# A new written order of steps and output products in a convolution and SwiGLU kernel

## The chip, the cores and the metric

The kernel runs on one core of a Trainium2 chip. A core has TensorE (matrix products, PE in the profile, with its weight loads as PEld), VectorE (DVE), ScalarE (ACT), GpSimd (POOL) and SyncE (SP), which here only issues transfers; each works through its own queue in order, and semaphores make one wait for another. The metric is the time of one execution on the device, in microseconds (us); lower is better.

## What is computed

The input x has 8 sequences of 4096 tokens with 192 channels. A causal convolution of 7 taps runs over each of 8 heads of 24 channels, its weights a softmax over the taps. Each token is then scaled by its root mean square and goes through a gated feed-forward layer with 1536 hidden channels, all in float32:

```python
w = np.exp(weight - np.max(weight, axis=-1, keepdims=True))
w = w / (np.sum(w, axis=-1, keepdims=True) + 1e-09)
out = np.einsum('hk,bskhg->bshg', w, x_unf)       # x_unf: the 7 last tokens of each token
rms = np.sqrt(np.mean(x * x, axis=-1, keepdims=True) + 1e-06)
xn = x / rms * rms_g
g = xn @ w_gate
val = xn @ w_val
return (silu(g) * val @ w_out).astype(np.float32)
```

## The kernel before

**Tiling.** The 32768 tokens are cut into 32 pairs of two tiles of 512 tokens. Pair 0 is computed plainly, with preparation of the weights in between; pairs 1 to 31 run through the loop at line 1437. What follows is about these 31.

**Fewer products by sums.** A 3 by 3 block product takes 15 products of sums of blocks where 27 would be plain, once for the two input projections and once for the output projection.
- *Chain* (`CHAINS`, line 801): 4 units of three hidden blocks, together 60 entries (unit, result v, product i), each for two halves h: h = 0 is the gate on partitions 0 to 63, h = 1 the value on partitions 64 to 127. One entry and half is one step, two matmul instructions of 64x512 (line 839). A pair has 120 such steps, 240 instructions. Their right-hand sides are the slots 0 to 15 of the tile `xa`: six fetched blocks and sums of them. Slots 12 and 13, and 10 and 14, hold sums for the other half of the partitions; `swap` (line 707) copies them there with two transfers each: `swA` from slots 6 and 11, `swB` from slots 8 and 9. In unit 0 the second entry reads slot 14, the fifth slot 12, the sixth slot 13.
- *Output products* (`OUTS`, line 93): 60 products named form.unit, for instance 13.3; 15 forms, 4 units. Each is 8 matmul instructions of 128x256 (line 1024). `LEFT` (line 934) says what each form reads: hidden blocks a to f, or the sums AB, CB, X and S, which are built up in place as the products go by (`SUMS`: abe adds e to AB between forms 8 and 13, abd adds d between forms 13 and 2).

**PSUM.** Eight banks, four per half. A chain result takes a bank when it starts, and gives it back when it has been read; the output accumulators N, R, K, C01 and C34 take banks in the same way. `F` steps fork a result: they copy one bank into another, from which a second sum goes on (`FORK`, line 808: F0 starts result 0 from result 1, F3 starts result 3 from result 5).

**The order.** `ORDER` (line 98) is a list written out by hand, one for all pairs. Its first letter is the engine: V and W VectorE, A ScalarE, G GpSimd, P VectorE with an operand staged in PSUM by the Ak step of the same name, Q a GpSimd transfer that adds as it lands, D a transfer. `p3` lets TensorE go on by three: chain steps first, then output products. A trailing `-` means that the step belongs to the pair before. Kinds of chain steps: S save, F fork, C, D, R, N sums, G Silu, M product of gate and value, with v, half and unit behind. `AF3.1.3` is so the fork of result 3, half 1, unit 3, on ScalarE. Of the output part: S8, S2 and others save a bank, D0 to D13 add saved banks, T0 to T5 transpose a finished accumulator into the output tile, `st0` and `st1` store it. The convolution of the pair after next runs along: `cv3_1` is tap 3 of third 1 (`part_tap`, line 462; the accumulator lies in the half that `SIDE` names), then sq, red, pre, pow, dup, bc, mul, place. X0 to X6 (line 714) build the sums of `xa` for the next pair: X2 makes slot 6, X3 slot 11, X5 slot 8, X6 slot 9, and `fetA`, `fetB` fetch its blocks.

**The last pair** has no successor, so `last` (line 1383) rewrites the order for it: the steps in `NEEDS` come as soon as what they need is there.

The order says in which sequence each engine meets its instructions. When one of them starts is settled by its engine's queue and by what it waits for.

Of the kernel before, what the change touches and what calls it, by code (L numbers as in the profile page):

```python
# [19 lines left out]
def kernel(  # L20
# [36 lines left out]
    PAIRS = B * NB  # L57
# [33 lines left out]
    PLACE = {'a': 3, 'b': 4, 'c': 5, 'd': 0, 'e': 1, 'f': 2}  # L91
    BANKS = {'K': 1, 'R': 0, 'N': 0, 'C01': 0, 'C34': 1}
    OUTS = (
        "6.2 11.2 6.0 6.1 11.0 11.1 6.3 4.0 11.3 4.1 4.2 9.1 14.0 14.3 14.1 4.3 9.2 9.0 9.3 8.1",
        "8.3 5.0 5.2 5.1 5.3 8.0 3.1 7.0 8.2 10.2 7.1 10.0 3.3 3.2 10.3 7.3 7.2 14.2 10.1 13.0",
        "1.1 13.2 1.2 12.0 12.3 12.2 12.1 13.3 13.1 3.0 1.3 1.0 0.3 0.0 0.1 2.0 0.2 2.1 2.3 2.2",
    )
    ORDER = (
        "Vcv4_1- p2 VT2- DswA- VD1- Vcv5_1- VT4- Vcv6_1- p1 AS2- VT1- AS40.0.0 p1 VD2- VT0- VT5-",
        "VD3- AS40.1.0 p1 AF0.0.0 Asq- p2 VT3- p1 VC.0.0 VF0.1.0 AS41.0.0 AS41.1.0 p1 VC.1.0 p2",  # L100
        "Vred- AS00.1.0 AS00.0.0 p2 VD5.0.0 AS42.0.0 p1 VD5.1.0 p4 VR0.0.0 Apre- p1 AS42.1.0 p1",
        "AS51.0.0 p1 AS51.1.0 p1 AF2.0.0 VR1.0.0 VR0.1.0 AG0.0.0 AG1.0.0 p2 VN.1.0 p2 VR1.1.0",
        "VR2.0.0 VR2.1.0 AF3.0.0 AF3.1.0 p3 AS44.0.0 p2 Gpow- AG2.0.0 VR3.0.0 AS44.1.0 p1 VR3.1.0",
        "p1 AS40.0.1 GM0.1.0 p1 GM2.1.0 AS40.1.1 VR5.1.0 AG4.0.0 Gdf.0 Adup- AF0.0.1 p1 AS41.0.1",
        "VR5.0.0 p2 AG3.0.0 VM4.1.0 VF0.1.1 p2 VC.0.1 AS41.1.1 p1 VC.1.1 AS00.0.1 p3 AG5.0.0",
        "GM1.1.0 GM3.1.0 VS00.1.1 AS42.0.1 AS42.1.1 p1 Vbc- VD5.0.1 p1 Qde.0 p1 VD5.1.1 AS51.0.1",
        "VR1.0.1 VR1.1.1 AS51.1.1 p2 Gmul- AF2.0.1 p1 Dload- p2 VR0.0.1 p2 AF2.1.1 p1 Gab.0 p2",
        "AG0.0.1 VR0.1.1 VR2.0.1 GM0.1.1 AF3.0.1 VR2.1.1 AF3.1.1 p3 AG2.0.1 p1 GM2.1.1 VS44.0.1",
        "p1 VR3.0.1 VR3.1.1 AS44.1.1 GM5.1.0 AS40.0.2 AS40.1.2 p1 AG4.0.1 VR5.0.1 p3 Gcb.0",
        "AF0.0.2 AG1.0.1 p1 VR5.1.1 VM4.1.1 VS41.0.2 VS41.1.2 p2 AF0.1.2 AG5.0.1 VC.0.2 Dplace-",  # L110
        "p1 VC.1.2 AS00.0.2 p1 GM1.1.1 p1 GM5.1.1 VS42.0.2 p1 Gdf.1 p1 AS00.1.2 p2 AG3.0.1 p1",
        "VD5.0.2 p1 AS42.1.2 VR1.0.2 VD5.1.2 AS51.0.2 p1 AF2.0.2 p1 AS51.1.2 VR1.1.2 VR0.0.2",
        "Gp4.0 Dst0- AF2.1.2 p2 AG1.0.2 GM3.1.1 p2 AG0.0.2 VR0.1.2 VF3.0.2 VR2.0.2 AF3.1.2 p1",
        "VR2.1.2 p1 AS44.0.2 p1 AG2.0.2 Qde.1 GM1.1.2 AS44.1.2 p3 AS40.0.3 VR5.0.2 GM0.1.2",
        "VR5.1.2 p1 GM2.1.2 p1 VR3.0.2 AS40.1.3 VR3.1.2 AG4.0.2 p2 AF0.0.3 Gdf.2 p1 VM4.1.2",
        "AF0.1.3 p1 VS41.0.3 p3 Gab.1 p1 AG3.0.2 p1 AS41.1.3 p1 VC.0.3 p1 AG5.0.2 AS00.0.3 p1",
        "VC.1.3 AS00.1.3 AS42.1.3 p1 GM3.1.2 p2 VS42.0.3 VD5.0.3 VD5.1.3 AS51.0.3 p1 VR1.0.3 p1",
        "AS51.1.3 p2 AF2.0.3 p1 GM5.1.2 Gde.2 VR1.1.3 p1 Gac.2 AG1.0.3 Dst1- VR0.0.3 VR0.1.3 p1",
        "AF2.1.3 p1 AS44.0.3 p1 AG0.0.3 GM1.1.3 VF3.0.3 p1 VR5.0.3 AF3.1.3 p1 AS44.1.3 VR2.0.3",
        "GM0.1.3 p1 DfetA VR2.1.3 VR3.0.3 AG2.0.3 GM2.1.3 WR3.1.3 Akp4.1 Pp4.1 p2 Gdf.3 AG5.0.3",  # L120
        "Gde.3 WR5.1.3 Akp4.2 AG4.0.3 p3 Akcb.1 VM4.1.3 AG3.0.3 Akab.3 p1 Pcb.1 p2 Pp4.2 VM3.1.3",
        "VM5.1.3 p1 Pab.3 p2 Akp9.2 p1 AF3 p1 Pp9.2 Gp9.1 p1 Akp4.3 p2 Acv0_0 Gcb.3 Gp9.0 Pp4.3",
        "Akp9.3 p1 Vcv1_0 p2 Qbe.0123 Pp9.3 Acv0_2 Vcv2_0 Vcv1_2 p1 Akbce.0 AF1 p2 AF0 Vcv3_0 p1",
        "Vcv2_2 p2 Vcv4_0 AS6 Pbce.0 p2 Qabe.13 Vcv5_0 p2 AS5 p1 Vcv3_2 Gbce.1 p2 AkX0 PX0 p2",
        "Akabe.0 p1 Gbce.23 Vcv6_0 p1 Vcv4_2 p1 Akabe.2 AS8 Pabe.0 Vcv5_2 Gbcf.01 Pabe.2 p1 AkX3",
        "p2 PX3 DfetB Vcv6_2 p3 AkX1 Gbcf.3 p1 Akbcf.2 AS7 p1 AkX4 PX1 Acv0_1 p2 Pbcf.2 p3 Qabd.0",
        "GX5 PX4 p1 VD7 p1 AkX6 AF4 p1 Vcv1_1 GX2 PX6 p2 Vcv2_1 p1 Gabd.13 AS13 p2 DswB p2 Gabd.2",
        "p2 VD6 Vcv3_1 VD0 VD13",
    )

    cst = ctx.enter_context(tc.tile_pool(name="cst", bufs=1))
# [4 lines left out]
    outs = ctx.enter_context(tc.tile_pool(name="outs", bufs=2))  # L136
# [785 lines left out]
    def out_sums():  # L922
# [4 lines left out]
            )  # L927
            yield

    SIDE = (1, 1, 1)  # L930
    regs = held[0 : 2 * NU] + [more[:, i] for i in range(2)]
    REG = {"AB": 0, "CB": 1, "X": 2, "S": 3}

# [22 lines left out]
        "T0": ("C0", 0, 0), "T1": ("C1", 0, 1), "T2": ("N", 0, 2),  # L956
        "T3": ("C3", 1, 0), "T4": ("C4", 1, 1), "T5": ("K", 1, 2),
    }

    class Pair:  # L960
        def __init__(self, p):
# [47 lines left out]
        def products(self):  # L1009
            for u, v, i in itertools.chain(*CHAINS):  # L1010
                for h in range(2):
                    self.units[u].product(h, v, i)
                    yield
            for w in " ".join(OUTS).split():
                n, u = (int(i) for i in w.split("."))
                src, b = LEFT[n]
                fresh = b in BANKS and b not in self.bk
                if fresh:
                    self.open(b, False)
                left = w_out(UNITS[n]) if n in UNITS else right(f"p{n}")  # L1020
                cols, to = self.form(src, u), self.part(b)
                for q in range(NQ):
                    i, a = divmod(q, 2)
                    nc.tensor.matmul(  # L1024
                        out=to[q * Q : (q + 1) * Q, :], lhsT=left[:, u, a],
                        rhs=cols[:, i * HALFT : (i + 1) * HALFT], start=fresh, stop=True,
                        skip_group_check=True, tile_position=(0, q * Q),
                    )
                yield
# [350 lines left out]
        "S2": "2",  # L1380
    }

    def last(order, outs):

        got, row, n = set(), [], 0
        todo = [w.split(".")[0] for w in outs]
        late = [w.strip("-") for w in order if w.strip("-")[1:] in NEEDS]

        def settle():
            more = True  # L1390
            while more:
                more = [w for w in late if got.issuperset(NEEDS[w[1:]].split())]
                for w in more[:1]:
                    late.remove(w)
                    row.append(w)
                    got.add(w[1:])

        def product(k):
            row.append("p1")
            todo.remove(k)  # L1400
            if k not in todo:
                got.add(k)
            settle()

        def products(count):
            nonlocal n
            for _ in range(count):
                n += 1
                k = outs[n - 121].split(".")[0] if n > 120 else ""
                if k:  # L1410
                    product(k)
                else:
                    row.append("p1")

        def other(w):
            if w[1:] not in NEEDS:
                row.append(w)
                got.add(w[1:])
                settle()

        for w in order:
            if w[-1] == "-":
                row.append(w)
            elif w[0] == "p":
                products(int(w[1:]))
            else:
                other(w)
        for w in order:
            if w[-1] == "-" and w[0] == "p":
                products(int(w[1:-1]))  # L1430
            elif w[-1] == "-" and ("." in w or w[1:-1] in FORKS or w[1:-1] in SNAP):
                other(w[:-1])
        assert not late and not todo
        return row

    past = None
    for p in range(1, PAIRS):
        now, steps = Pair(p), 0
        if p == PAIRS - 1:
            order = last(order, " ".join(OUTS).split())  # L1440
        for w in order:
            if w[0] == "p" and w[-1] == "-":
                for _ in range(int(w[1:-1]) if past else 0):
                    next(past.line)
                continue
            if w[0] == "p":
                for _ in range(int(w[1:])):
                    next(now.line)
                    steps += 1
                    if p == 1 and steps == 40:  # L1450
                        w_signs(3, 4)
                    if p == 1 and steps in (36, 40, 44, 48):
                        next(wsum)
                continue
            eng, name = w[0], w[1:]
            of = now
            if name[-1] == "-":
                name, of = name[:-1], past
            if of:
                of.do(eng, name)  # L1460
            elif name == "mul":
                next(norm2)
            elif name == "place":
                done(place(2))
        past = now
# [28 lines left out]
```

## Time and profile before

| what | us |
|---|---|
| median of 3 runs | 2583.95 (2583.94 to 2584.12) |
| the profiled execution | 2585.07 |
| its span | 2583.2 |
| one pair, chain start to chain start | 79.0 |
| TensorE busy | 2568.1 (99%) |
| DVE busy | 2405.4 (93%) |
| POOL busy | 2056.8 (80%) |
| ACT busy | 1957.8 (76%) |

The span runs from the first instruction to the last. Pair after pair takes the same 79.0 us, so that one pair stands for all: chain starts lie at 1706.31 and 1785.33 in the stretch that is read below. Matmuls are pipelined and their ends are modelled: a busy TensorE need not be at its peak. The weight load of a matmul waits for what the matmul waits for, so that waits that are not seen on PE can be seen on PEld.

### The profile page before, as it was taken

The page shows a single profiled execution, that of the slowest core. Times are in us where ns is not written, and L with a number is a line of the kernel's source. Part 1 is how long each engine was busy: PE and PEld are TensorE (multiplying, and loading weights), DVE is VectorE, ACT ScalarE, POOL GpSimd, SP SyncE. Part 2 cuts the span into 40 slices and gives each one's busy share as a digit, 9 for nine tenths or more (in the row PEclk, how much of TensorE's full clock was granted, in tenths as well). Part 3 has the DMA queues.
Part 4 walks back from the last instruction along what each step waited for, and adds up shares of the span by engine and source line. Part 5 has one row for each costly group of instructions (what it writes and reads, how often), then busy time and mean ns, then how long its engine had stood idle before and what let it go on. Part 6 is the DMA issues. An engine that isn't in the chain of part 4 may idle for free.

```text
span 2583.2 us, 61873 instructions
## 1 busy us (share of the span) xinstructions
PE 2568.1 (99%) x23114; PEld 1637.6 (63%) x23114; DVE 2405.4 (93%) x4009; ACT 1957.8 (76%) x3749; POOL 2056.8 (80%) x1581
## 2 busy tenths in 40 slices
PE   8999999999999999999999999999999999999998
PEld 6857666666666666666666666666667566666665
DVE  8799999999999999999999999999999999999976
ACT  6588777787777887778877778777788777787765
POOL 3897778977778877779777788777887777978777
PEclk9999999999999999999999999999999999999999
DMA  6444556445545445554455554455644555544442
GB/s 145 92 87 86 107 101 116 96 95 103 108 98 114 98 87 108 99 117 95 96 99 108 102 112 96 87 110 99 121 93 97 93 108 108 108 95 92 95 99 46
DMA packets 535411, 259.33 MB, mean 100 GB/s; under 512 B 458566, under 2 KB 462278, under 8 KB 531142
## 3 DMA queue, kind: packets, MB, share of 16 engines
q1 hardware_dynamic: 507860, 182.03, 34.4%
q0 software_dynamic: 26288, 73.15, 15.4%
q8 instruction: 182, 2.98, 0.5%
q14 instruction: 119, 0.97, 0.1%
q10 hardware_dynamic: 962, 0.20, 0.0%
HBM read 100.10 MB, written 49.55 MB: 58 GB/s over the span
## 4 chain that ended last, share of the span: by engine, by line
PE 97%; POOL 1%; DMA 1%; issue 0%; ACT 0%; SPq 0%; DVE 0%; ACTq 0%; POOLq 0%; DVEq 0%
PE ps L839 63%; PE ps L1024 31%; PE ps L1156 2%; DMA xa<-xa 0%; POOL xa L737 0%; PE ps L415 0%; POOL wo_sb L332 0%; POOL wf L366 0%; DMA xa<-xd 0%; PE ps L581 0%; SPq L686 0%; POOL xa L331 0%; POOL yn L548 0%; DMA xd<-yn 0%; POOL xa L726 0%
## 5 line engine op out<-in xcount | busy, mean ns | idle before, releaser
L839 PE MATMUL ps<-xa,wf 64*128 64x512 f32 x7440 | 1646.3, 592 | 2.1 <-DMA xa<-xa 0.9
L839 PEld LDWEIGHTS ps<-xa,wf 64*128 64x128 f32 x7440 | 1063.0, 186 | 572.0 <-issue 118.0
L791 ACT ACTIVATE tile<-ps 128x512 f32<-128x512 f32 (+1 forms) x770 | 433.3, 570 | 200.4 <-PE ps L1024 109.2
L791 ACT ACTIVATE tls<-ps 128x512 f32<-128x512 f32 (+1 forms) x687 | 386.3, 567 | 168.2 <-PE ps L1024 104.0
L791 ACT ACTIVATE ps<-ps 128x512 f32<-128x512 f32 (+1 forms) x713 | 387.8, 547 | 122.8 <-PE ps L1024 92.3
L893 POOL TENSOR_TENSOR ht<-ht,tile 128x512 f32<-128x512 f32 x305 | 387.9, 1281 | 92.5 <-ACT tile L885 78.9
L1024 PE MATMUL ps<-ht,x 128*32 128x256 f32 x5952 | 390.4, 380 | 0.2 <-DVE ps L1091 0.2
L893 POOL TENSOR_TENSOR ht<-ht,tls 128x512 f32<-128x512 f32 x253 | 321.9, 1279 | 64.1 <-ACT tls L885 56.2
L478 DVE SCALAR_TENSOR_TENSOR ps<-xh,tp,ps 128x512 f32<-128x512 f32 x450 | 322.5, 748 | 1.0 <-DMA xd<-yn 0.9
L1024 PEld LDWEIGHTS ps<-ht,x 128*32 128x32 f32 x5952 | 191.3, 110 | 145.3 <-issue 23.5
L1024 PE MATMUL ps<-early,x 128*32 128x256 f32 x3968 | 254.0, 379 | 0.0
L873 DVE TENSOR_TENSOR tile<-ps,tile 128x512 f32<-128x512 f32 x347 | 236.8, 685 | 14.9 <-ACT tile L791 7.6
L528 POOL TENSOR_TENSOR r<-r,nhalf 128x8 f32<-128x8 f32 x29 | 48.4, 1669 | 241.1 <-ACT r L524 241.1
L873 DVE TENSOR_TENSOR ht<-ps,tile 128x512 f32<-128x512 f32 x325 | 221.6, 685 | 9.8 <-ACT tile L791 6.3
L1047 POOL TENSOR_TENSOR early<-early,ht 128x1024 f32<-128x1024 f32 x93 | 225.9, 2495 | 3.5 <-PE ps L1024 3.0
L885 ACT ACTIVATE tile<-tile 128x512 f32<-128x512 f32 x347 | 215.7, 625 | 2.0
L873 DVE TENSOR_TENSOR tls<-ps,tls 128x512 f32<-128x512 f32 x273 | 185.4, 684 | 10.0 <-PE ps L839 3.9
L1024 PEld LDWEIGHTS ps<-early,x 128*32 128x32 f32 x3968 | 129.1, 110 | 85.0 <-ACT ps L791 5.1
L885 ACT ACTIVATE tls<-tls 128x512 f32<-128x512 f32 x273 | 168.8, 624 | 1.7
L873 DVE TENSOR_TENSOR ht<-ps,tls 128x512 f32<-128x512 f32 x233 | 159.0, 684 | 6.2 <-ACT tls L791 3.5
L1069 POOL TENSOR_TENSOR early<-ht 128x512 f32<-128x512 f32 x124 | 159.8, 1288 | 2.6
L1024 PE MATMUL ps<-early,wo_sb 128*32 128x256 f32 x2232 | 143.5, 379 | 0.0
(165 smaller groups left out, 3627.8 us busy)
## 6 DMA issues: line engine op xcount, KB each, us to landing
xa<-xd SPq DMA_DIRECT2D x186, 256.0 KB, 4.3
xa<-xa SPq DMA_DIRECT2D x124, 256.0 KB, 4.2
ht<-ht POOLq DMA_DIRECT2D x31, 1024.0 KB, 7.7
xd<-yn SPq DMA_DIRECT2D x248, 96.0 KB, 2.5
out_dram<-o_sb SPq DMA_DIRECT2D x246, 96.0 KB, 2.0
xh<-in_x_dram SPq DMA_DIRECT2D x192, 105.0 KB, 3.6
xa<-xd SPq DMA_DIRECT2D x124, 128.0 KB, 4.5
more<-ht POOLq DMA_DIRECT2D x62, 256.0 KB, 3.3
```

The costliest lines, as they stand in the source:

```text
L478: nc.vector.scalar_tensor_tensor(out=dst, in0=xk, scalar=w, in1=at, op0=ALU.mult, op1=ALU.add)
L528: nc.gpsimd.tensor_tensor(out=r, in0=r, in1=nhalf[:, 0 : nb * NR], op=ALU.pow)
L791: nc.scalar.activation(out=dst, in_=src, func=AF.Copy, scale=float(s))
L839: nc.tensor.matmul(out=self.new(v, h, True) if first else self.old(v, h), lhsT=wf[self.u][HALF[h], WAT[i], :], rhs=x_op(XOP[i], h), start= ...
L873: nc.vector.tensor_tensor(out=dst, in0=self.old(v, h), in1=t[:], op=plus(s))
L885: nc.scalar.activation(out=t[:], in_=src[:], func=AF.Silu)
L893: engine[eng].tensor_tensor(out=self.hv(v), in0=src, in1=t[:], op=ALU.mult)
L1024: nc.tensor.matmul(out=to[q * Q : (q + 1) * Q, :], lhsT=left[:, u, a], rhs=cols[:, i * HALFT : (i + 1) * HALFT], start=fresh, stop=True, s ...
L1047: nc.gpsimd.tensor_tensor(out=dst, in0=a, in1=b, op=ALU.add)
L1069: engine[eng].tensor_tensor(out=dst, in0=a, in1=b, op=ALU.add)
L1156: nc.tensor.matmul(out=bank(h, bks[h])[:], lhsT=wf[u][HALF[h], AT[h][k] * NF + f, :], rhs=xb[HALF[h], g, k, :], start=(k == 0), stop=(k == ...
```

## The change

`ORDER`, `OUTS` and `SIDE` are replaced, and the last pair gets an end of its own.

- The loop's seam moves: 59 of a pair's 60 output products, and the steps among them, are now written ahead with a `-`, in the next round. The sequence on TensorE stays chain, then output products; the products come in another sequence.
- Steps change engines. F0.1.0 goes from VectorE to ScalarE, F3.0.3 from VectorE to ScalarE, S44.0.3 from ScalarE to VectorE; X0 and X3 go from VectorE to GpSimd, X5 from GpSimd to VectorE, X6 from VectorE to GpSimd. Some single sums become one sum of two units and the reverse. VectorE has one 512-column step less, ScalarE two less.
- X2 now stands behind two sums abd.0 and abd.1 in GpSimd's queue; before, the sums abd stood behind X2. `swA` follows X2.
- `LAST` ends the last pair's products with form 0 (form 2 before). `last` now puts sums and saves ahead of the products that need them (`LEAD`, `HELD`).

The diff, cut to the parts around the seam, the chain's end and the last pair:

```diff
@@ -91,41 +91,43 @@
     OUTS = (
...
-        "1.1 13.2 1.2 12.0 12.3 12.2 12.1 13.3 13.1 3.0 1.3 1.0 0.3 0.0 0.1 2.0 0.2 2.1 2.3 2.2",
...
+        "5.1 3.0 5.0 5.3 5.2 8.0 10.1 8.1 3.1 3.3 10.2 8.2 8.3 7.1 7.0 7.3 7.2 13.2 1.2 10.0 10.3",
+        "12.2 1.3 3.2 13.3 1.0 13.0 13.1 1.1 12.3 12.0 12.1 2.3 2.0 0.0 2.2 2.1 0.3 0.1 0.2",
     )
+    LAST = "7.2 13.2 13.3 13.0 13.1 1.2 10.0 10.3 12.2 1.3 3.2 1.0 1.1 12.3 12.0 12.1 2.3 2.0 2.2 2.1 0.0 0.3 0.1 0.2"
     ORDER = (
-        "Vcv4_1- p2 VT2- DswA- VD1- Vcv5_1- VT4- Vcv6_1- p1 AS2- VT1- AS40.0.0 p1 VD2- VT0- VT5-",
-        "VD3- AS40.1.0 p1 AF0.0.0 Asq- p2 VT3- p1 VC.0.0 VF0.1.0 AS41.0.0 AS41.1.0 p1 VC.1.0 p2",
...
-        "AF2.1.3 p1 AS44.0.3 p1 AG0.0.3 GM1.1.3 VF3.0.3 p1 VR5.0.3 AF3.1.3 p1 AS44.1.3 VR2.0.3",
-        "GM0.1.3 p1 DfetA VR2.1.3 VR3.0.3 AG2.0.3 GM2.1.3 WR3.1.3 Akp4.1 Pp4.1 p2 Gdf.3 AG5.0.3",
...
-        "p2 PX3 DfetB Vcv6_2 p3 AkX1 Gbcf.3 p1 Akbcf.2 AS7 p1 AkX4 PX1 Acv0_1 p2 Pbcf.2 p3 Qabd.0",
-        "GX5 PX4 p1 VD7 p1 AkX6 AF4 p1 Vcv1_1 GX2 PX6 p2 Vcv2_1 p1 Gabd.13 AS13 p2 DswB p2 Gabd.2",
-        "p2 VD6 Vcv3_1 VD0 VD13",
+        "AG2.0.3- Gp4.1- VR5.0.3- VM2.1.3- AG4.0.3- p1- GM1.1.3- p3- Gdf.3- p2- VR3.0.3- VR5.1.3-",
+        "Akp9.1- AG5.0.3- Akcb.0- VM4.1.3- AG3.0.3- Pcb.0- Akcb.2- Gde.3- WR3.1.3- Akp9.0- p1-",
+        "GM5.1.3- p1- Pcb.2- Pp9.0- p1- Akp4.3- AF3- Pp9.1- p1- Akp9.2- Gcb.3- Akab.3- VM3.1.3-",
+        "p1- Pp9.2- p1- Pab.3- p2- Pp4.3- Gp9.3- Qbe.0123- p1- Acv0_0- p2- AF0- Vcv1_0- Vcv2_0-",
+        "AS6- AkX1- Akbce.0- p1- Vcv3_0- p2- GX0- GX3- p1- Gbce.1- p1- PX1- p1- Gbce.3- AF1- p3-",
+        "Pbce.0- Vcv4_0- p1- Vcv5_0- Qabe.01- AS5- AkX4- Acv0_1- p6- Vcv6_0- PX4- p1- Vcv1_1- p1-",
+        "Akbce.2- Gabe.2- Qbcf.01- Acv0_2- Gabe.3- Pbce.2- Vcv1_2- Vcv2_1- p1- AS8- p2- Akbcf.2-",
+        "AS7- p1- Gbcf.3- Pbcf.2- p2- AkX5- p2- Qabd.2- Vcv3_1- Vcv4_1- PX5- p2- Akabd.3- Vcv2_2-",
+        "GX6- p2- VD0- Vcv3_2- p2- Pabd.3- Gabd.0- AS13- p2- AF4- Gabd.1- Vcv4_2- VD7- GX2- p1-",
+        "Vcv5_1- DswB- VD13- p1- Vcv6_1- p4- Vcv5_2- p2- VD6- AS2- p1 Vcv6_2- VD2- p1 VT2- p1",
+        "Asq- VD1- VT5- p1 AS40.0.0 p1 VT1- VT4- VT0- AS40.1.0 VD3- DswA- VT3- VC.0.0 p1 AF0.0.0",
+        "p1 AF0.1.0 p1 AS41.0.0 p1 AS41.1.0 p2 VC.1.0 Vred- p2 Dload- AS00.0.0 AS00.1.0 VD5.0.0",
...
+        "Gp4.0 AF2.1.3 p2 WR0.1.3 AG0.0.3 p1 GM3.1.2 VM0.1.3 AF3.0.3 VS44.0.3 AF3.1.3 Gab.2 Gde.2",
+        "AS44.1.3 p4 VR2.0.3 AG1.0.3 WR2.1.3 DfetB Gp4.2 p1",
     )
@@ -927,7 +929,7 @@
-    SIDE = (1, 1, 1)
+    SIDE = (0, 1, 1)
@@ -957,6 +959,10 @@
+    def out_steps(p):
+        every, end = " ".join(OUTS).split(), LAST.split()
+        return every if p < PAIRS - 1 else every[: -len(end)] + end
+
@@ -1380,6 +1386,8 @@
+    LEAD, HELD = {"13": "abe", "2": "abd"}, {"13": "S8", "2": "S13"}
+
@@ -1418,18 +1427,30 @@
+        def lead(k, u):
+            for i, w in enumerate(left):
+                name, *of = w[1:].split(".")
+                ahead = len(of) == 1 and name.lstrip("k") == LEAD.get(k) and u in of[0]
+                if ahead or name and name == HELD.get(k):
+                    left[i] = ""
+                    other(w)
+
```

## The prediction

> **What bounds the kernel now.** I read the page's busy times, then the chain of waits in order of time, then the timeline around the two seams of one pair.
>
> ```profile
> PE 2568.1 (99%) x23114; PEld 1637.6 (63%) x23114; DVE 2405.4 (93%) x4009; ACT 1957.8 (76%) x3749; POOL 2056.8 (80%) x1581
> ```
>
> By this row TensorE is the bound and idles for 15 us in all. The chain of waits, between 1700 and 1790 us, stays on it too:
>
> ```profile
> 1706.38 50.96 PE ps L839 x234
> 1757.34 0.04 issue
> 1757.38 1.98 PE ps L839 x6
> 1759.36 26.04 PE ps L1024 x480
> ```
>
> A pair is 240 chain instructions in 52.98 us and 480 output instructions in 26.04: 79.02. Is that TensorE's own pace? The timeline of PE alone has an undisturbed stretch:
>
> ```profile
> 1719.42 37.07 PE L839 MATMUL ps<-xa,wf 64*128 64x512 f32 x171
> ```
>
> The last of the 171 takes 0.59, so (37.07 - 0.59) / 170 = 0.2146 us each. 240 at that pace are 51.50 us: the chain loses 1.48 us per pair that the busy row hides, 46 us over 31 pairs. In sentences of its own: the Trainium skill (Trainium Kernel Development and Optimization, Performance Expectations) calls matmul busy time a bad metric because matmuls are pipelined. By the busy row no change could gain over 15 us; the trace agrees with the page.
>
> The loss is seen on the weight loads. Undisturbed, 0.19 to 0.24 us lie between two of them. At the chain's start (C = 1706.31 in this pair) and at its end:
>
> ```profile
> 1709.87 0.69 DVE L795 COPY ps<-ps 128x512 f32<-128x512 f32 x1
> 1710.61 0.30 PEld L839 LDWEIGHTS ps<-xa,wf 64*128 64x128 f32 x4 [0.57 <-DVE ps L795]
> ```
>
> ```profile
> 1755.72 0.60 ACT L791 ACTIVATE tls<-ps 128x512 f32<-128x512 f32 x1 [0.56 <-PE ps L839]
> 1756.22 0.62 ACT L885 ACTIVATE tile<-tile 128x512 f32<-128x512 f32 x1
> 1756.74 0.59 ACT L791 ACTIVATE ps<-ps 128x512 f32<-128x512 f32 x1
> ...
> 1757.38 0.30 PEld L839 LDWEIGHTS ps<-xa,wf 64*128 64x128 f32 x4 [0.86 <-ACT ps L791]
> ```
>
> The first wait is for fork F0.1.0, the second for F3.1.3, behind the save S44.0.3 and a Silu in ScalarE's queue. By the waits view both come back from pair to pair; of the first there are 31, one per pair, 16.9 / 31 = 0.55 each:
>
> ```profile
> PEld ps L839 <- ACT ps L791: 53.6, 103, 0.9
> ...
> PEld ps L839 <- DVE ps L795: 16.9, 31, 0.6
> ```
>
> The excess over 0.24 is 0.33 and 0.62 us. The two halves run side by side, one pass per 0.429 us (two times 0.2146), so a late half can lose a whole pass: 0.43 for the first. Together that is about 1.05 of the 1.48; I take the rest as the seams' own.
>
> **The change, part by part.** Loads first. Per pair VectorE has one 512-column step less (they follow each other at 0.60 us) and ScalarE two less (0.5 each), on rows where both have room; GpSimd's sums and triggers, added up at 1.23 for one unit, 2.33 for two and 0.6 to 1.1 for a trigger, come to 0.9 us less. TensorE's instructions are the same in number and kind. So nothing becomes a bound by its load, and the sum is made at the seams.
>
> *Fork F0.1.0*, from VectorE to ScalarE. It needs the bank that T3 gives back. Before, VectorE ran T1, D2, T0, T5, D3, T3 after the last tap (T3 ended at C+2.48), then C.0.0, then the fork, which ended at C+4.25. Now all short steps (0.33 to 0.35 each, 0.45 where one needs the one before) follow the last tap, but they are the same 13. VectorE runs without a break from the chain's end to there, so T3's time follows from the work: one step less, -0.60; six taps that now follow right on the tap they depend on, so that the end of 0.75 and not the pace of 0.66 counts, about +0.12 each; the stretch begins some 0.2 later, behind a Silu that M0.1.3 waits for. That is +0.3: T3 at C+2.8, the fork on ScalarE (0.60) at C+3.45. TensorE wants it at 4 entries of 0.858 plus 0.1, C+3.54. I take the whole 0.43 back; bounds 0 and 0.86 (two passes of one half).
>
> *F3.1.3*: S44.0.3 leaves ScalarE's queue ahead of it, and F3.0.3 comes in. Without the wait of 0.56 for S44.0.3's product, the Silu can start at about 1755.2, F3.0.3 0.52 later, F3.1.3 at 1756.2, 0.5 earlier than the 1756.74 above. I take 0.38 of the 0.62; bounds 0 and 0.62.
>
> *New waits at the start.* T5 gives back the bank that the second entry's upper half wants at C+0.96. T5 now stands fourth after the last tap; with T3 at C+2.8, five short steps behind it, it ends at C+0.95: between 0 and 0.3 late.
>
> *The swap swA*, on the path through GpSimd, SP and the transfer. Before:
>
> ```profile
> 1777.76 2.96 POOL L737 TENSOR_TENSOR xa<-xa 128x512 f32<-128x512 f32 x2
> 1780.76 2.38 POOL L1047 TENSOR_TENSOR early<-early,ht 128x1024 f32<-128x1024 f32 x1
> ```
>
> X5 and X2 were done at 1780.72, 4.6 us ahead of the next chain. Now GpSimd has, from Gdf.3 at about 1.0 us into the output products: df 1.37, de 1.23, M5 1.36, cb 1.36, p9 1.23, a trigger 0.88, X0 1.80 (X3 needs it, and it takes 1.72), X3 1.25, two bce 2.46, a trigger 0.75, abe 1.23, a trigger 0.75, abe 1.23, bcf 1.23, a trigger 0.61, X6 1.25, abd.0 and abd.1 2.46, X2 1.72: 24.2 us, so X2 ends 25.2 after the start of the 26.04, at C-0.85. Behind it on SP wait swA's two transfers and then the eight loads of x, which have a pair's time. The transfers issue at C-0.8 and, 0.7 later, at C-0.1. For line 712 the trace gives
>
> ```profile
> DMA to landing us min/median/max: 3.2/4.2/6.5
> ```
>
> with four in a row; two are to come behind each other now. The second lands between C+3.1 and C+6.4, at the median C+4.1; slot 12 is wanted at C+3.54. Two in a row are nearer to the shorter end; I take 3.7, C+3.6. T5's lateness and this one overlap, so one term of +0.25 stands for both; bounds 0 and, with 6.5, 2.9. In sentences of its own: the Trainium skill (DMA: Bandwidth & Descriptors, Anatomy of one DMA) fits a GpSimd-issued transfer with 2.0 us plus bytes over 436 GB/s, an estimate of 2.6 us for 256 KB, and the swap would never be late (-0.56 would become -0.66 or so). No landing on this row is under 3.2, so the measurement decides.
>
> *Sum of the seams*: -0.43 - 0.38 + 0.25 = -0.56 per pair, 30 times: -16.8.
>
> *The end.* The tail before:
>
> ```profile
> 2575.38 1.48 PE L1024 MATMUL ps<-early,wo_sb 128*32 128x256 f32 x24
> 2576.93 0.38 ACT L791 ACTIVATE tile<-ps 128x256 f32<-128x256 f32 x1 [4.36 <-PE ps L1024]
> ...
> 2578.62 0.45 DVE L1037 STREAM_TRANSPOSE o_sb<-ps 128x256 f32<-128x256 f32 x1
> 2579.10 0.88 ACTq L1110 DMA_DIRECT2D out_dram<-o_sb  x2
> ```
>
> S2, two sums and two transposes end 2.2 us after the last product (2576.86). With form 0 last, they start four products (1.73) earlier, and T4 comes behind them, one step of 0.35 to 0.44: it ends 0.9 after the last product, -1.3. But in `LAST` 13.3 comes six products (2.6 us) after 8.2, and abe.3 needs abe.2 1.23, a trigger 0.75 and its own 1.28 after 8.2: 0.8 late with the hand-over. -0.5 in all.
>
> Total -17.3. On the profiled execution (2585.07 with 2583.2 of span) that is 2567.8; it lies 1.1 over the median, which I forecast: 2583.95 - 17.3 = **2566.7**.
>
> **Rivals.**
> - *More comes back*: all of 0.43 + 0.62 and no new wait, 30 times 1.05 and the end: 2552. For it: POOL and SP may run ahead of my sums. Against: T5 has no room.
> - *No change*: a gain at one seam is lost at the next, since VectorE runs without a break through the output products and its end fixes T3, T5 and the forks. Then only the end's 0.5 stays: 2583.5. Against: both forks move off VectorE's or a save's queue.
> - *Slower*: swA lands late in each pair. The seams give 0.81; from a landing of 4.45 us after issue (C+4.35) on, the wait for slot 12 costs more than that. At 5.0 it is 1.36 late and the pair 0.55 longer: 2600. For it: X2 ends 3.7 us later than before, and the median of 4.2 is not far; against: fewer transfers queue ahead.
> - *The rewritten last pair stalls further*: it is one pair, and twice my 0.8 would make 2567.5, inside the range.
>
> **How the numbers follow.** My forecast 0.64 (its own range 2558 to 2577), more 0.12, none 0.09, slower 0.15. The range 2554 to 2588 leaves out the upper part of the slower case and the far end of the first rival. The bound of 0.2% is 5.2 us, about what a measurement of this kernel can tell from no change: the first two cases are faster, 0.76, the third the same, 0.09, the last slower, 0.15.
>
> **What would show it.** Right: the chain's stretch between output stretches falls from 52.98 to about 52.4, chain start to chain start to 78.5; PEld waits for DVE L795 fall well under 31 long ones; the last store issues about 0.9 us after the last product. Wrong: PE or PEld wait for the transfers of line 712 in most pairs; or the chain keeps its 52.98 with another engine named before the same two steps. What would undo the forecast is a landing of swA beyond 4.45 us, or a wait in mid-chain, where I priced nothing because each step there has several entries of cover.

## The result and the profile after

| what | before | after |
|---|---|---|
| median of 12 runs each, us | 2584.19 (2583.75 to 2585.37) | 2590.28 (2588.47 to 2591.76) |
| span of the profiled execution, us | 2583.2 | 2587.7 |
| chain of a pair, median, us | 52.98 | 53.00 (shortest 52.32) |
| output stretches of 30 pairs, beyond 26.04 us each, summed | 0.2 | 5.6 |
| last pair, first output product to the end of the span, us | 32.9 | 37.1 |

The changed kernel is slower by the factor 1.0023, interval 1.0014 to 1.0032; the prediction was 2566.7. The busy row of the page of the changed kernel (engine, us, share of the span, instructions) says nothing of that:

```profile
PE 2559.4 (99%) x23114; PEld 1718.5 (66%) x23114; DVE 2370.3 (92%) x3980; ACT 1929.6 (75%) x3689; POOL 2020.8 (78%) x1641
```

TensorE is busy for 9 us less, and the span is 4.5 us longer. The waits view of TensorE does show it (who waited, for whom: us in total, times, longest):

```profile
PE ps L841 <- DMA xa<-xa: 7.1, 17, 1.5
PE ps L1030 <- DMA early<-ht: 3.2, 4, 1.2
...
PE ps L1030 <- POOL early L1075: 2.4, 2, 1.5
PE ps L1030 <- DVE o_sb L1043: 2.4, 1, 2.4
```

The first row had 2 waits and 0.9 us before. It is the transfer of the swap. The other three rows are new; they lie in the output products.

The two spans can be split by the starts of the chains and output stretches. The first chain starts 0.1 earlier and is 1.5 shorter; the other 30 chains are shorter by 3.5 in all (mean 53.045 before, 52.928 after); the output stretches are longer by 5.4, the last pair's end by 4.2. That makes -5.1 + 9.6 = +4.5. So the chains' gain is 3.5 where the prediction had 16.8, and two losses of about 5 each have taken more than that away.

The chain of waits of the changed kernel in the pair whose chain starts at C = 439.67 (start, us, what), with SP's second swap transfer in it:

```profile
438.84 0.59 SPq L714
439.43 0.05 issue
439.49 4.22 DMA xa<-xa
443.71 0.14 issue
443.84 48.94 PE ps L841 x224
```

GpSimd finished X2 at C-0.86, and SP issued at C-0.83 and C-0.18, as forecast (C-0.8 and C-0.1). But the second transfer took 4.22 us and landed at C+4.04, and the entry wanted at C+3.54 began at C+4.17. The prediction took 3.7 for this landing. The remaining 224 instructions follow in 48.94 with no further wait named.

In the last pair, PE's timeline of the changed kernel has two gaps (start, us, engine, line, operation; in brackets the idle time before and what ended it):

```profile
2569.17 1.50 PE L1030 MATMUL ps<-early,x 128*32 128x256 f32 x24 [1.52 <-POOL early L1075]
...
2579.50 3.50 PE L1030 MATMUL ps<-ht,x 128*32 128x256 f32 x32 [2.35 <-DVE o_sb L1043]
```

The first is 13.3 behind the sum abe.3. The second is the whole of form 0, and VectorE's timeline shows what it waits for:

```profile
2578.47 0.40 DVE L1097 TENSOR_TENSOR ps<-ps,tile 128x256 f32<-128x256 f32 x1
2578.91 0.45 DVE L1043 STREAM_TRANSPOSE o_sb<-ps 128x256 f32<-128x256 f32 x1
2583.06 0.45 DVE L1043 STREAM_TRANSPOSE o_sb<-ps 128x256 f32<-128x256 f32 x1 [3.71 <-PE ps L1030]
```

D3 and then T3, which reads C3; form 0 writes C4. Both are halves of one PSUM bank, C34. The products stand still until T3 has read its half; T4 (2583.06) comes after them. That the shared bank is what ties them together is read from the code; no run puts the two halves in separate banks.

The products of form 0 also run at half pace: 32 instructions take 3.50, where 32 in a row took 1.91 shortly before. The granted clock, last but two in the rows of the windows view (stretch, length, busy us of PE, PEld, DVE, ACT, POOL, clock, DMA share, GB/s), falls in the wait:

```profile
2576.00:2578.00 2.00, 1.15 (x24) 0.41 (x15) 0.69 (x2) 0.38 (x1) 0.00 (x0) 1.00 0.78 187
2578.00:2579.50 1.50, 0.00 (x0) 0.03 (x1) 1.28 (x4) 0.00 (x0) 0.00 (x0) 0.94 0.06 13
2579.50:2581.00 1.50, 1.50 (x16) 0.87 (x20) 0.00 (x0) 0.00 (x0) 0.00 (x0) 0.50 0.00 0
```

So behind the wait of 2.35 another 1.6 is lost here. In all 1.52 + 2.35 + 1.6, less 1.7 that PE's end now lies nearer to the end of the span, make 3.8 of the 4.2 that the last pair lost. The 1.6 does not always come with the wait: four of the kernels below have the same wait of 2.35 to 2.36, and in the profile of one (swap_other_first) the clock falls as well, to 0.50, and the 32 instructions take 3.28; in the other three (swap_undo_f0, swap_undo_f3, load_late) it stays at 1.00, and they take 1.93, as here in load_late:

```profile
2571.58 1.93 PE L1030 MATMUL ps<-ht,x 128*32 128x256 f32 x32 [2.36 <-DVE o_sb L1043]
```

### The profile page after: what moved, and what is told of

Same layout as the page of the kernel before. It is cut to its first block, busy times and chain, and to the rows that moved or that the text cites. A ratio compares the mean times of both kernels' runs of the same rounds, so it can differ in the third digit from the quotient of the medians.

```text
span 2587.7 us, 61947 instructions
## 1 busy us (share of the span) xinstructions
PE 2559.4 (99%) x23114; PEld 1718.5 (66%) x23114; DVE 2370.3 (92%) x3980; ACT 1929.6 (75%) x3689; POOL 2020.8 (78%) x1641
## 4 chain that ended last, share of the span: by engine, by line
PE 84%; POOL 6%; DMA 5%; issue 3%; DVE 1%; ACT 1%; SPq 1%; POOLq 0%; DVEq 0%; ACTq 0%
PE ps L841 60%; PE ps L1030 22%; DMA xa<-xa 3%; POOL early L1075 2%; PE ps L1162 2%; POOL xa L739 2%; DMA early<-ht 1%; POOL early L1073 1%; DVE ps L480 1%; SPq L714 0%; DMA xa<-xd 0%; ACT early L413 0%; DMA x<-in_x_dram 0%; DVE early L1075 0%; POOL wo_sb L334 0%
## 5 line engine op out<-in xcount | busy, mean ns | idle before, releaser
L841 PEld LDWEIGHTS ps<-xa,wf 64*128 64x128 f32 x7440 | 1148.4, 186 | 481.6 <-issue 130.1
L793 ACT ACTIVATE ps<-ps 128x512 f32<-128x512 f32 x744 | 405.3, 550 | 137.7 <-PE ps L1030 86.6
L793 ACT ACTIVATE tls<-ps 128x512 f32<-128x512 f32 (+1 forms) x653 | 360.2, 563 | 125.2 <-PE ps L1030 59.2
L1030 PE MATMUL ps<-ht,x 128*32 128x256 f32 x5952 | 402.5, 381 | 2.5 <-DVE o_sb L1043 2.4
L480 DVE SCALAR_TENSOR_TENSOR ps<-xh,tp,ps 128x512 f32<-128x512 f32 x450 | 334.0, 750 | 5.1 <-DMA xd<-yn 0.9
L895 POOL TENSOR_TENSOR ht<-ht,tls 128x512 f32<-128x512 f32 x222 | 284.2, 1290 | 55.1 <-ACT tls L887 53.0
L1075 POOL TENSOR_TENSOR early<-early,ht 128x512 f32<-128x512 f32 x217 | 301.7, 1534 | 11.7 <-PE ps L1030 11.6
L739 POOL TENSOR_TENSOR xa<-xa 128x512 f32<-128x512 f32 x125 | 204.6, 1637 | 4.1 <-DMA xa<-xd 1.6
L875 DVE TENSOR_TENSOR ht<-ps,tile 128x512 f32<-128x512 f32 x290 | 195.5, 679 | 0.0
L747 ACT COPY ps<-ht 128x512 f32<-128x512 f32 x217 | 127.6, 588 | 73.4 <-DVE xa L739 42.2
```

Source lines behind the costliest of these rows:

```text
L480: nc.vector.scalar_tensor_tensor(out=dst, in0=xk, scalar=w, in1=at, op0=ALU.mult, op1=ALU.add)
L739: e.tensor_tensor(out=d, in0=a, in1=unstage(staged, i, b), op=ALU.add)
L747: nc.scalar.copy(out=bank(*at)[:], in_=src)
L793: nc.scalar.activation(out=dst, in_=src, func=AF.Copy, scale=float(s))
L841: nc.tensor.matmul(out=self.new(v, h, True) if first else self.old(v, h), lhsT=wf[self.u][HALF[h], WAT[i], :], rhs=x_op(XOP[i], h), start= ...
L875: nc.vector.tensor_tensor(out=dst, in0=self.old(v, h), in1=t[:], op=plus(s))
```

## The experiments

All times are medians beside runs of the kernel before on the same chip (three chips, 2584.04 to 2584.58). For the chains, one table made from the traces: the start of the k-th of a pair's 240 chain instructions, less C and less 0.42925 us for every two (the undisturbed pace, 2 times 0.2146), median over pairs 2 to 30, in us. Entry 4, the first to read slot 12, begins at k = 16; k = 240 is the first output product, so that a chain lasts 51.51 plus the last column.

```
kernel              k=16   k=18   k=30   k=46   k=230  k=232  k=236  k=240
before              0.10   0.44   0.54   0.54   0.53   0.53   0.95   1.47
after               0.73   0.80   0.80   0.88   0.87   0.87   0.99   1.51
swap_other_first    0.10   0.10   0.10   0.18   0.17   0.17   0.29   0.81
swap_undo_f0        0.10   0.48   0.56   0.56   0.55   0.55   0.55   1.07
swap_undo_f3        0.15   0.15   0.15   0.18   0.17   0.55   0.65   0.84
load_late           0.27   0.35   0.35   0.42   0.41   0.41   0.55   1.07
bef_forks           0.10   0.80   0.90   0.90   0.90   0.90   0.90   1.70
bef_forks_sq        0.10   0.10   0.27   0.29   0.45   0.46   0.46   1.39
```

**The swap alone.** Entry 4's waiting half reads what one of swA's two transfers brings; in the changed kernel it is the one that issues second.

```diff
-        for rows, other in ((LOW, UPP), (UPP, LOW)):
+        ways = ((UPP, LOW), (LOW, UPP)) if act == "swA" else ((LOW, UPP), (UPP, LOW))
+        for rows, other in ways:
             nc.sync.dma_start(out=xa[other, to], in_=xa[rows, at])
```

> The changed kernel with one edit: swA issues its upper-to-lower transfer first and its lower-to-upper second. The entry that waits at C+3.54 reads slot 12 in the lower half, which only the transfer that is now first fills; the upper halves are read four entries later at the earliest. Theory (the landing of swA's second transfer is what holds the chain at 53.05): the transfer that counts issues 0.64 us earlier, at C-0.83, and lands at about C+3.5; waits of PE for xa by DMA fall from 17 (7.1 us) to a few, the usual chain goes from 53.05 to about 52.4, and the time falls by some 12 to 17 us, to 2573 to 2578. Rival 1 (another step, T5 or fork F0.1.0, is late by as much and was only hidden behind it): PE or PEld name DVE or ACT at the same place, chain 52.9 to 53.1, time within 3 us of 2590. Rival 2 (the landing is set by what else is on the DMA engines then, not by its issue): same count of DMA waits, same time.

Measured: 2570.44 (2570.09 to 2572.9), ratio to before 0.995, interval 0.9936 to 0.9964. That is 19.8 us from the changed kernel for the order of two transfers, and both rivals fall. The theory's 12 to 17 were for the chains: in the two traces the chains from the second on are shorter by 17.6 of the 19.0 by which the span falls; the output stretches, at which the edit does not aim, give 2.1. One wait of 0.4 us for the swap is left, and 27 of the chains from the second on take 52.32, one of them here in the chain of waits of this kernel:

```profile
1693.45 52.32 PE ps L842 x240
1745.77 26.04 PE ps L1031 x480
```

52.32 and 26.04 make 78.36, which is what the prediction's seams without a new wait come to within 0.15 (79.02 - 0.81 = 78.21).

**What makes the landing long.** The eight loads of x are put behind another group of transfers on SP.

```diff
-... Vred- p2 Dload- AS00.0.0 ...
+... Vred- p2 AS00.0.0 ...
-... VR5.0.1 Dplace- AS40.0.2 ...
+... VR5.0.1 Dplace- Dload- AS40.0.2 ...
```

> The changed kernel, swA's transfers in its own order, with one edit: the eight loads of x, which issue on SP right behind swA's two transfers (C+0.5 to C+7.9), stand behind the four transfers of Dplace, some 22 us later. Theory A (the second transfer of swA takes about 4.3 us and the first 3.4 because the loads of x, issued 0.65 us behind it, share its time): it lands at C+3.5, the chain falls from 53.05 to about 52.4, 12 to 18 us, 2572 to 2578. Theory B (it takes longer because it runs behind the first transfer, whatever follows): the chain keeps 53.05 and the time 2590 within 3 us.

Measured: 2579.97 (2578.65 to 2581.8), ratio 0.9982, interval 0.9974 to 0.9991. In this kernel SP's timeline has the loads 28 us after the swap (start, us, queue, line):

```profile
2331.36 1.24 SPq L714 DMA_DIRECT2D xa<-xa  x2
2354.03 5.24 SPq L688 DMA_DIRECT2D xd<-yn  x8
2359.37 6.68 SPq L158 DMA_DIRECT2D xh<-in_x_dram  x8
```

and the waits of TensorE for the swap become

```profile
PE ps L841 <- DMA xa<-xa: 3.0, 4, 0.9
```

Between the two theories: entry 4 begins 0.46 us sooner (0.73 to 0.27 in the table), three quarters of what was lost there; 10 of the 20 us come back. So the loads behind the swap delay its second transfer by about half a microsecond, and the rest of its lateness, 0.17, is there without them. The landings say the same: by the landing events of the traces (medians over pairs 2 to 30) the second transfer takes 4.23 us from its issue in the changed kernel and 3.78 here, the first 3.30 and 3.26.

**Fork F0.1.0 undone**, with the swap mended, so that nothing else holds entry 4.

```diff
-        "p1 AF0.1.0 p1 AS41.0.0 ...
+        "p1 VF0.1.0 p1 AS41.0.0 ...
```

> The changed kernel with swA's transfers in the other order, and fork F0.1.0 back on VectorE behind C.0.0. Theory (step 2 of the prediction: this fork on ScalarE is worth a pass of one half, 0.43): the chain goes from 52.32 to 52.75, 30 times 0.43 = 13 us, 2583. Rival 1 (VectorE reaches it in time in the new order): 2570. Rival 2 (C.0.0 and the copy come a whole pass later than before, too): 53.1, 2596.

Measured: 2577.22 (2576.25 to 2578.16), ratio 0.9973, interval 0.9963 to 0.9984: 6.8 us, half of the theory's 13. The table says why. At k = 30 the chain is late by 0.56 and not 0.10, which is the pass of 0.43 that the theory has. But between k = 30 and k = 236 the later kernel loses nothing, where the other loses 0.08 and then 0.12. A late start gives the later steps time, and 0.26 is left at k = 240.

**Fork F3.1.3 undone**, in the same way.

```diff
-... AF3.0.3 VS44.0.3 AF3.1.3 ...
+... VF3.0.3 AS44.0.3 AF3.1.3 ...
```

> The changed kernel with swA's transfers in the other order, and at the chain's end S44.0.3 back on ScalarE ahead of F3.1.3, F3.0.3 back on VectorE. Theory (step 2: F3.1.3 behind the save is 0.4 to 0.5 us later): the chain goes from 52.32 to 52.7, 11 us, 2582. Rival (the end of the chain has room here, because the start is no longer late): within 3 us of 2570.

Measured: 2572.04 (2571.08 to 2572.35), ratio 0.9952, interval 0.9939 to 0.9966: the rival's time. But the edit does not make F3.1.3 late. In the median pair it ends at C+50.39, against C+50.36 with the swap mended alone. In the kernel before, the Silu stood between the save S44.0.3 and the fork; in the new order it is done ahead of the save, and ScalarE has time for the save (C = 1696.29):

```profile
1744.61 0.63 ACT L888 ACTIVATE tls<-tls 128x512 f32<-128x512 f32 x1
1745.60 0.60 ACT L794 ACTIVATE tile<-ps 128x512 f32<-128x512 f32 x1 [0.36 <-PE ps L842]
1746.09 0.59 ACT L794 ACTIVATE ps<-ps 128x512 f32<-128x512 f32 x1
```

What is late, by 0.38 more at k = 232, is the other fork, F3.0.3: on VectorE it ends at C+50.29, on ScalarE it ended at C+49.43. TensorE's weight loads name it in every pair:

```profile
PEld ps L842 <- DVE ps L796: 21.2, 31, 0.8
```

In the last column only 0.03 of this remains: from k = 236 on the mended kernel loses 0.52 and this one 0.19. What this fork loses, the chain's last steps lose anyway. What F3.1.3 is worth by itself this run does not show.

**The forks alone in the old order.**

```diff
-... AF0.0.0 Asq- p2 VT3- p1 VC.0.0 VF0.1.0 AS41.0.0 ...
+... AF0.0.0 Asq- p2 VT3- p1 VC.0.0 AF0.1.0 AS41.0.0 ...
-... AS44.0.3 p1 AG0.0.3 GM1.1.3 VF3.0.3 p1 VR5.0.3 ...
+... AG0.0.3 GM1.1.3 AF3.0.3 p1 VS44.0.3 p1 VR5.0.3 ...
```

> The kernel before with two edits alone: fork F0.1.0 on ScalarE in place of VectorE, and at the chain's end F3.0.3 on ScalarE and S44.0.3 on VectorE, which takes the save out of ScalarE's queue ahead of F3.1.3. Orders of sums, taps, output products and transfers stay those of before, so swA keeps its 3 us of room. Theory (two late forks cost about 0.8 us per pair, and what the changed kernel lost against it came from swA and the output steps): the chain goes from 52.98 to 52.2 to 52.4, times 30: -17 to -24 us, 2560 to 2567. Rival 1 (the gain at the start is taken by T5 or swA, which are next): chain 52.6 to 53, -12 at most. Rival 2 (each fork only shifts its wait to another engine): no change, 2584.

Measured: 2593.25 (2592.77 to 2594.97), ratio 1.0035, interval 1.0023 to 1.0048, slower than any of the three had it. ScalarE's timeline in this kernel, pair with C = 1711.59:

```profile
1713.72 0.61 ACT L791 ACTIVATE ps<-ps 128x512 f32<-128x512 f32 x1
1714.23 1.48 ACT L494 ACTIVATE yn<-y 128x1536 f32<-128x1536 f32 x1
1715.60 0.60 ACT L791 ACTIVATE ps<-ps 128x512 f32<-128x512 f32 x1
```

The second copy is F0.1.0. It stands behind the square of y, which in the old order cannot start before the last tap, and ends at C+4.61; on VectorE it ended at C+4.25. In the next kernel it goes ahead of the square:

```diff
-... AF0.0.0 Asq- p2 VT3- p1 VC.0.0 VF0.1.0 AS41.0.0 ...
+... AF0.0.0 p2 VT3- p1 AF0.1.0 Asq- VC.0.0 AS41.0.0 ...
```

> The kernel before with the fork edits of bef_forks, but with F0.1.0 ahead of the square of y on ScalarE; in bef_forks it stood behind that square (1.48 us) and ended at C+4.6, later than VectorE's at C+4.25. Theory (the fork has only to end by C+3.54, and the rest of before's order leaves swA room): F0.1.0 ends at C+3.2 to 3.4, entry 4 is on time, the chain falls from 52.98 to about 52.4, -17 us, 2567. Rival (the square, 0.6 us later, and S41.0.0 behind it take the fork's place as the late step): chain 52.8 to 53.3, 2579 to 2594.

Measured: 2584.77 (2583.31 to 2585.82), ratio 1.0002, interval 0.9994 to 1.0011: the rival. The fork now ends at C+3.33 in the median (C+3.22 in the pair shown, C = 1705.95) and entry 4 is on time (0.10 at k = 18), but the square and the saves behind it come 0.5 us later:

```profile
1708.08 1.09 ACT L791 ACTIVATE ps<-ps 128x512 f32<-128x512 f32 x2
1709.08 1.48 ACT L494 ACTIVATE yn<-y 128x1536 f32<-128x1536 f32 x1
1710.46 0.59 ACT L791 ACTIVATE tls<-ps 128x512 f32<-128x512 f32 x1
```

and by k = 230 the chain is late by 0.45. At the chain's end F3.1.3 is done at C+50.29 and not at C+51.02, and the 0.42 that the kernel before loses between k = 232 and 236 are gone; but the first output product then starts late, and 0.93 is lost from k = 236 to 240, where the kernel before loses 0.52. So both moves won something at their place and next to nothing at the chain's end. In the new order the taps, and so the square, come ahead of F0.1.0, and there its move pays.

**The last pair.** Two other ends of its products.

```diff
-    LAST = "7.2 13.2 13.3 13.0 13.1 1.2 10.0 10.3 12.2 1.3 3.2 1.0 1.1 12.3 12.0 12.1 2.3 2.0 2.2 2.1 0.0 0.3 0.1 0.2"
+    LAST = "7.2 13.2 1.2 13.0 13.1 1.3 13.3 12.2 1.0 1.1 12.3 12.0 12.1 2.3 2.0 2.2 2.1 10.0 10.3 3.2 0.0 0.3 0.1 0.2"
```

> The changed kernel with another order of the last pair's last 24 products: 13.3 stands six products behind 13.2, and 10.0, 10.3 and 3.2 stand between the last product of form 2 and the first of form 0. Theory (the last pair loses 2.35 us because form 0's products wait for transpose T3 of the same PSUM bank, and 1.5 us because 13.3 waits for abe.3): three products (1.3 us) and the T3 chain run side by side, so 1.3 to 2.3 of the 2.35 and most of the 1.5 come back; the span falls by 2.5 to 3.8 us, the pairs before stay as they are, about 2587. Rival (the wait is for T3 but of another reason, as the output tile of the store): the wait of 2.35 stays, -1.5 at most.

```diff
+    LAST = "7.2 13.2 1.2 10.0 10.3 13.0 13.1 13.3 12.2 1.3 3.2 1.0 1.1 12.3 12.0 12.1 0.0 0.3 0.1 0.2 2.3 2.0 2.2 2.1"
```

> The changed kernel with the last pair ending on form 2 again (form 0 ahead of form 2), and 13.3 five products behind 13.1. Theory (same bank): form 0 comes ahead of T3, so the wait of 2.35 us for T3 is gone; behind the last product stand S2, two sums and two transposes again, so PE's end to the end of the span grows from 4.7 to 6.0 to 6.4. Net -0.7 to -1.1 there and -1.5 for abe.3: about -2.3, 2588. Rival (form 0 at the end is worth its 1.7 us and the wait has another cause, which stays): +0.2 or slower, 2590 or more.

Measured: last_far 2588.98 (2586.45 to 2592.03), ratio 1.0017, interval 1.0008 to 1.0025; last_two 2588.27 (2587.05 to 2591.72), ratio 1.0016, interval 1.0008 to 1.0025. The totals overlap with the changed kernel's; the stretch from the last output products to the end of the span is clearer: 37.07 in the changed kernel (35.5 where the clock stays up, as in load_late), 34.99 and 34.52 in these. The wait for abe.3 is gone in both, but waits of 1.25 and 0.73 for a transfer stand near its place. In last_far PE still waits for a transpose:

```profile
2579.00 2.37 PE L1030 MATMUL ps<-ht,x 128*32 128x256 f32 x40 [1.73 <-DVE o_sb L1043]
```

and VectorE has two of them just before:

```profile
2577.73 0.40 DVE L1097 TENSOR_TENSOR ps<-ps,tile 128x256 f32<-128x256 f32 x1
2578.17 0.78 DVE L1043 STREAM_TRANSPOSE o_sb<-ps 128x256 f32<-128x256 f32 x2
```

The 40 instructions are not form 0 alone (32) but 3.2 as well. It writes C0, and 10.3, just ahead of it, finished C1, the other half of the bank C01, so that T1 comes between them, at VectorE's end of the queue. By this reading the experiment ran into the same thing in another bank; nothing separate was run for that bank. After a wait of 1.73 the granted clock stays at 1.00, and 40 instructions take 2.37. In last_two, form 0 comes ahead of T3, its wait is for the fork F4 and 0.49 us, and the wait for a transpose is gone:

```profile
2576.93 1.93 PE L1030 MATMUL ps<-ht,x 128*32 128x256 f32 x32 [0.49 <-ACT ps L793]
2578.68 1.91 PE L1030 MATMUL ps<-early,wo_sb 128*32 128x256 f32 x32
```

The time from PE's end to the end of the span is 6.37 there and 4.70 in the changed kernel. So ending on form 0 does save 1.7 us behind the last product, and costs 2.35 ahead of it, with the half clock on top in some executions.

**Swap and last pair together**, with 1.3 and 3.2 put where last_two still waited: `LAST = "7.2 13.2 1.2 10.0 10.3 1.0 1.1 13.3 13.0 13.1 12.2 12.3 1.3 12.0 12.1 3.2 0.0 0.3 0.1 0.2 2.3 2.0 2.2 2.1"`.

> The changed kernel with swA's transfers in the other order and another end of the last pair: form 0 ahead of form 2, 13.3 to 13.1 five products later, 1.3 and 3.2 between. Theory (swap: 20 us, measured; last pair: no wait for T3's bank, for abe.3, abe.01 or bcf.01): the stretch from the last output products to the end of the span falls from 36.9 to 33.3 to 34.5, time 2567 to 2568. Rival (sums on GpSimd for form 2, which now follow later on form 13, hold the end): 36 or more, time 2569 to 2571.

Measured: 2569.19 (2567.43 to 2569.76), ratio 0.994, interval 0.9928 to 0.9953. The last stretch is 33.45, in the theory's range, 3.4 less than in swap_other_first, whose profile has 1.4 of half clock in it; the time is only 1.25 less, which the rival had. Its reason is not the rival's: in the profiled execution the other output stretches are longer by 2.8 us (6.3 beyond 26.04 against 3.5).

**The output stretches.** Three of them, of 27.2 to 27.4, wait near their end as here in swap_last (first PE's timeline, then GpSimd's):

```profile
829.04 0.61 PE L1031 MATMUL ps<-ht,x 128*32 128x256 f32 x8
830.65 1.07 PE L1031 MATMUL ps<-early,wo_sb 128*32 128x256 f32 x16 [1.00 <-DMA early<-ht]
```

```profile
822.21 2.81 POOL L1076 TENSOR_TENSOR early<-early,ht 128x512 f32<-128x512 f32 x2
824.68 1.17 POOL L1074 DMA_DIRECT2D early<-ht  x1
```

Product 2.2 waits for Qabd.2, which issued at 824.68 behind the sums abe.3 and bcf.3 and landed just before 830.65, some 6 us later.

```diff
-        "AS7- p1- Gbcf.3- Pbcf.2- p2- AkX5- p2- Qabd.2- Vcv3_1- ...
+        "AS7- p1- Qabd.2- Gbcf.3- Pbcf.2- p2- AkX5- p2- Vcv3_1- ...
```

> swap_last with one edit more: the transfer Qabd.2 issues ahead of the GpSimd sum bcf.3 and not behind it, 1.2 us earlier, after the output step has finished 13.2. Theory (the output stretches that run to 26.5 and 27.4 wait for this transfer at product 2.2, which has 4.5 us for a landing of 3.6 to 6.1): the pairs with 27.2 to 27.4 go to 26.04 to 26.2, the excess of all output stretches from 6.3 us to about 3 (the pair with 27.84 waits ahead of this step, and stays), time 2565 to 2567. Rival (it queues behind the transfer of bcf.01 and lands when it did): no change, 2569.

Measured: 2566.35 (2565.34 to 2566.97), ratio 0.9928, interval 0.9915 to 0.9942. The three pairs go to 26.04, and the same pair's products run through:

```profile
827.70 0.61 PE L1031 MATMUL ps<-ht,x 128*32 128x256 f32 x8
828.13 1.05 PE L1031 MATMUL ps<-early,wo_sb 128*32 128x256 f32 x16
829.00 1.48 PE L1031 MATMUL ps<-ht,x 128*32 128x256 f32 x24
```

The sum of the excess goes from 6.3 to 4.5, less far than expected: other pairs now have 0.3 to 0.7, and the one with 27.84 has 28.45. The rival is half right: the landing of Qabd.2 has a median of 5.4 us here against 4.05 in swap_last, so that in the usual pair it lands no earlier (23.1 and 23.0 us after the first output product); what is gone are the landings of 5.9 to 6.1 in those three pairs. This is the fastest of the kernels that ran, 18.2 us below the kernel before in the same runs.

## Why the prediction was wrong, step by step

- **The chain's hidden loss** was read rightly. With the swap mended, the chain goes from 52.98 to 52.32 at unchanged instructions, though the busy row had only 15 us of idle time for the whole span and 20 us came back between two kernels that differ by the order of two transfers.
- **Fork F0.1.0, -0.43.** The size at its place is right, and so is the timing: T3 ends at C+2.78 and the fork at C+3.48 (forecast 2.8 and 3.45), and the lateness of 0.44 at k = 18 and 0.54 at k = 30 falls to 0.10. Undone in the mended kernel it costs 0.26 at the end of the chain, since later steps have less room when the start is on time. In the old order the forks' moves together bring nothing, or cost 9 us where F0.1.0 stands behind the square. The prediction had the term as independent of the order around it.
- **F3.1.3, -0.38.** The size is near, the cause is open. The gain at the chain's end is 0.30 (0.94 lost from k = 232 to 240 before, 0.64 with the swap mended), and the fork starts at C+49.77 and not at C+50.43 (forecast: 0.5 earlier), though 0.36 of these 0.66 is only that the chain is less late by then. But the exchange of the save S44.0.3 for F3.0.3 in ScalarE's queue is not what brings it: with the exchange taken back, the fork ends only 0.03 later. Whether it is the Silu, which no longer waits behind the save, or another step of the new order was not tried. That both forks together made 0.81 in the forecast and 0.66 in the traces is partly luck, since the two are not independent terms.
- **T5 and swA, +0.25: the step that failed.** T5 ended at C+0.98 (forecast 0.95) and cost nothing (with the swap mended, 0.10 at k = 16, as before). The queue sum was right to 0.1 us. The landing was taken as 3.7 after the second issue, as nearer to the short end of 3.2 to 6.5 because fewer transfers queue ahead; it was 4.22 in the pair shown, 4.23 in the median. (The fit that the prediction quotes from the Trainium skill, DMA: Bandwidth & Descriptors, Anatomy of one DMA, gave an estimate of 2.6 and is further off; the measurement decides.) What counted was the queue behind: eight loads of x, issued from 0.65 us later on, are worth 0.46 at entry 4; without them the landing is 3.78, close to what was taken. The prediction names these loads in the same paragraph and lets them wait, without asking whom they delay. The term was about 0.7 in the usual pair (1.51 less 0.81 at k = 240), nearly all that the forks brought.
- **The slower rival** was this mechanism. It asked for 4.45 before the gain is gone; at the measured 4.2 the seams still gave 0.12 per pair in the mean, and the chains alone would have made the kernel faster by 5.1 us. That it came out slower is the work of the next two points.
- **The end, -0.5.** The tail became shorter as forecast (1.3 forecast, 1.69 measured from PE's end to the span's end). The wait for abe.3 was 1.52 and not 0.8. And form 0's wait of 2.35 for T3 was not foreseen: the two halves of C34 were treated as two accumulators. That the clock then falls to half, as in this profile and one other of the five with this wait, the loop of the trace before could not show: no wait of TensorE there is longer than 1 us from the second chain on. -0.5 became +4.2, of which 1.6 is the clock.
- **The output products** were taken to keep their 26.04. This term was put at nothing without a reason. Five stretches ran longer, 5.6 us in all: the prediction looked at the transfer of the swap and at no other, although the change moves Qabe.01, Qbcf.01 and Qabd.2 as well. For three of them Qabd.2 is shown to be the cause. The longest (28.39; the same pair in each kernel of the new order) begins with a gap in GpSimd's queue ahead of Qbcf.01, here in the changed kernel:

```profile
1930.40 0.85 POOL L1051 DMA_DIRECT2D early<-ht  x1
...
1935.29 0.87 POOL L1051 DMA_DIRECT2D early<-ht  x1 [2.44 <-issue]
```

  In the other pairs this gap is 0.47. What fills it is open.

The range ended at 2588, 2.3 us short. The bounds of the swap's term alone, up to 2.9 per pair, reach far beyond that; for the output products no bound was set at all, and for the last pair only twice 0.8.

## What to carry to other kernels

Of several transfers issued in a row, find the one that the first reader waits for, issue it first, and count what issues behind it as well as ahead: here that is 20 us of 2590 for two swapped lines. A wait that is removed in a tight chain is worth what is left of it at the chain's end, and a fork moved to another engine is worth what stands ahead of it there; try both with the rest of the new order in place. When an order is rewritten, list all transfers it moves with the time that each has to land, and count accumulators that share a PSUM bank as one when products and transposes follow each other closely.

## What was not expected of the hardware

- Transfers issued behind a transfer lengthened it here: with eight loads right behind the swap, its second transfer of 256 KB landed 4.23 us after issue, and 3.78 when the loads went elsewhere; entry 4 then began 0.46 us sooner.
- A wait of TensorE of 2.35 us halved its granted clock in two profiles (0.94, then 0.50, until about 3.2 us after the wait in the changed kernel) and left it at 1.00 in three others; after 1.73 and 1.52 it stayed at 1.00. The Trainium skill (TensorE: Matmul & The Clock Gate, Part 1: The HAM clock gate) has the half clock after an idle window of about 3.4 us; two traces have it after less.
- A GpSimd-issued transfer of 256 KB (Qabd.2) has a median landing of 4.1 us from its issue in the changed kernel, but takes 5.2 to 6.1 in the three pairs that stalled for it, the sixth, ninth and twelfth of the loop; the first two of these stall in most kernels of the new order.
- One pair of 31 has a GpSimd gap of 2.44 us before an issue, the 23rd of the loop in each of the nine kernels of the new order, and nothing is named that it waits for.
